# Hardware loops on VectorE, ScalarE and GpSimd, and attention probabilities staged four pairs at a time, in a decode kernel that streams a key and value cache

## The chip, the cores and the metric

One core of one Trainium2 chip runs the whole program. The metric is the device time in microseconds of one execution; where several runs are given, the median.

## The reference

Two token rows go through a gated mix of a cached attention (32 heads of 128, 4096 cached positions, batch 2) and a small feed-forward network. Cut to what matters:

```python
q = (x @ wq)                                      # [2, 32 heads, 1, 128]
scores = einsum("bhqd,bhkd->bhqk", q, k) * Dh**-0.5
p = softmax(scores)
o = einsum("bhqk,bhkd->bhqd", p, v)               # k, v: [2, 32, 4096, 128] bf16, 67 MB each
a = o.reshape(B, Sq, Hq * Dh) @ wo
b = relu(x @ w1) @ w2
return g * a + (1 - g) * b                        # g = sigmoid(sum(x * gate_w))
```

The caches are 134 MB of the 145 MB that the kernel reads; each byte is used once.

## The kernel before

One queue, issued by SyncE, loads everything in order: `wq`, `w1`, `w2`, then 32 loads of K of 2 MB (two heads of one batch row, called a pair here), 32 loads of V, and last `wo` in five pieces. K and V go through four slots:

```python
for n in range(64):
    waits = []
    if n >= NSLOT:                                   # NSLOT = 4
        prev = n - NSLOT
        waits.append(f"T_{prev}_7" if prev < 32 else f"pv_{prev - 32}")
    load(f"ld_kv_{n}", kv_sb[:, n % NSLOT, :, :], kv_in(n), waits=waits, sem=f"slot{n % NSLOT}")
```

In the K stage PE transposes each pair (64 blocks, 8 to a PSUM bank), VectorE and ScalarE evict the banks (copy them from PSUM to SBUF), and PE forms scores. In the V stage the probabilities are copied to SBUF (staged), PE multiplies them with V, and VectorE normalises. PE's two stages are already hardware loops. The other engines' instructions are written out in full:

```python
def evac(i):                                         # called for each of the 32 pairs
    p = i % PER
    for q in range(8):
        ...
        w = [f"T_{i}_{q}"] + ([f"sc_{i - NKT}"] if i >= NKT else [])
        if q in (1, 3, 5):
            P.add("act", lambda e, dst=dst, src=src: e.activation(out=dst, in_=src, func=ACT.Copy), waits=w, ...)
        else:
            P.add("dve", lambda e, dst=dst, src=src: e.tensor_copy(out=dst, in_=src), waits=w, ...)

def stage_p(i):                                      # the same, for each pair
    ...
    for hh in range(2):
        P.add("dve", lambda e, hh=hh: e.tensor_copy(out=pst[64 * hh:64 * hh + 64, p, :, hh], in_=src[:, :, 2 * hp + hh]),
              waits=[f"pt_{g}", "c_ps"] + ([f"pv_{i - PER}"] if i >= PER else []),
              signal=f"pst_{i}" if hh else None, sem=f"ps{p}")

def o_norm(i):
    ...
    P.add("dve", lambda e: e.tensor_tensor(out=oT[:, g, 2 * hp:2 * hp + 2], in0=o_col(i % PER), in1=rg[...], op=ALU.mult),
          waits=[f"pv_{i}", f"rg_{g}"], signal=f"oT_{i}", sem=f"on{i % PER}")
```

VectorE's program has 405 instructions, 107 of them waits that stand as instructions of their own; ScalarE's has 113, GpSimd's 95, PE's 1951.

Of the kernel before, what the change touches and what calls it, by code (L numbers as in the profile page):

```python
# [37 lines left out]
class _Prog:  # L38
# [7 lines left out]
    def __init__(self, nc):  # L46
        self.nc = nc
        self.streams = {e: [] for e in self.ENGINES}
        self.sems = {}
        self.marks = {}  # L50
        self.loops = []

    def sem(self, name):
        if name not in self.sems:
# [2 lines left out]

    def add(self, engine, fn, waits=(), signal=None, sem=None, inc=1):
        op = _Op(fn, waits, signal, sem or engine + "_ev", inc)
        if engine == "pe" and self.loops:  # L60
            self.loops[-1].ops.append(op)
        else:
            self.streams[engine].append(op)

    def begin_loop(self, n):
        loop = _Loop(n)
        (self.loops[-1].ops if self.loops else self.streams["pe"]).append(loop)
        self.loops.append(loop)

    def end_loop(self):  # L70
        self.loops.pop()

    def _count(self, op, name, counts):
        if name is None:
# [40 lines left out]
    def emit(self, engine, eng, items=None, iv=None, total=1):  # L115
        vals = {}
        for it in self.streams[engine] if items is None else items:
            if isinstance(it, _Loop):
                with eng.Fori(0, it.n) as k:
                    self.emit(engine, eng, it.ops, k if iv is None else iv * it.n + k, total * it.n)  # L120
                continue
            if iv is None:
                waits = list(self._needs(it.waits).items())
            else:
                waits = []
                for s, a, b in self._linear(it, total):
                    if b and (a, b) not in vals:
                        vals[(a, b)] = eng.snap(iv * b + a)
                    waits.append((s, vals[(a, b)] if b else a))
            for s, v in waits:  # L130
                eng.wait_ge(self.sem(s), v)
            ins = it.fn(eng)
            if it.signal is not None:
                ins.then_inc(self.sem(it.sem), it.inc)


def bass_gated_mix__gqa_block_cached__dense_activation_relu__decode_kernel(
# [43 lines left out]
    negM = sb("negM", [128, 2], f32)  # L181
    l4 = sb("l4", [128, 2], f32)
    lm = sb("lm", [128, 32], f32)
    rinv = sb("rinv", [128, 2, 32], f32)
    rg = sb("rg", [128, 2, 32], f32)
    oT = sb("oT", [128, 2, 32], b16)
    oA = sb("oA", [128, 2, 32, 4], b16)
    os_sb = sb("os_sb", [128, 32, 2], b16)
    f_sb = sb("f_sb", [98, 128], f32)
# [21 lines left out]
        return bank(ACC, 0, 128, 32 * c, 32 * c + 2)  # L211

    def o_col(p):
        return bank(4 + p % 2, 256 + 2 * p, 2)

    def p_place(r):

# [27 lines left out]
    for n in range(64):  # L245
        waits = []
        if n >= NSLOT:
            prev = n - NSLOT
            waits.append(f"T_{prev}_7" if prev < 32 else f"pv_{prev - 32}")
        load(f"ld_kv_{n}", kv_sb[:, n % NSLOT, :, :], kv_in(n), waits=waits, sem=f"slot{n % NSLOT}")  # L250
    WO_CUTS = (0, 16, 24, 28, 30, 32)
    for k in range(5):
# [58 lines left out]
    def T(p, qs):  # L311
        for q in qs:
            for rr in range(8):
                r = 8 * q + rr

                def waits(t, q=q):
# [4 lines left out]
                    elif p:  # L321
                        w.append(f"ev_{i - 1}_{q + 4}")
                    return w + (["qm_0", "qm_1", "f_sb"] if p == 0 and q == 0 else [])

                P.add("pe", lambda e, q=q, rr=rr, r=r: e.transpose(bank16(4 + q % 4, rr * 128, 128), kv_sb[:, p, r, :], ident16[:, :]),  # L325
                      waits=waits if rr == 0 else [],
                      signal=(lambda t, q=q: f"T_{PER * t + p}_{q}") if rr == 7 else None)

    def Sc(p):
        for c in range(8):  # L330
            for hh in range(2):
                def waits(t, c=c):
                    i = PER * t + p
                    return ([f"qst_{i}"] if c == 0 else []) + ([f"ev_{i}_{c}"] if c >= 4 else [])

                P.add("pe", lambda e, c=c, hh=hh: e.matmul(  # L336
                    S_chunk(p % 2, c), lhsT=qst[:, p, hh, :], rhs=kt_sb[:, p % NKT, 8 * c:8 * c + 8, 64 * hh:64 * hh + 64],
                    start=False, stop=True, tile_position=(0, 32 * (c % 4)), skip_group_check=True),
                    waits=waits if hh == 0 else [],
                    signal=(lambda t: f"sc_{PER * t + p}") if (c, hh) == (7, 1) else None)  # L340

    def evac(i):
        p = i % PER
        for q in range(8):
            src = bank16(4 + q % 4, 0, 1024).rearrange("p (r c) -> p r c", r=8)
            dst = kt_sb[:, p % NKT, 8 * q:8 * q + 8, :]
            w = [f"T_{i}_{q}"] + ([f"sc_{i - NKT}"] if i >= NKT else [])
            if q in (1, 3, 5):
                P.add("act", lambda e, dst=dst, src=src: e.activation(out=dst, in_=src, func=ACT.Copy), waits=w,  # L349
                      signal=f"ev_{i}_{q}", sem=f"ev{p}{q}")  # L350
            else:
                P.add("dve", lambda e, dst=dst, src=src: e.tensor_copy(out=dst, in_=src), waits=w, signal=f"ev_{i}_{q}", sem=f"ev{p}{q}")  # L352

    def stage_q(i):
        p = i % PER
        P.add("pool", lambda e: e.tensor_copy(out=qst[:, p, :, :], in_=qmask[:, 32 * (i % 2) + i // 2 * 2:32 * (i % 2) + i // 2 * 2 + 2, :]),  # L356
              waits=[f"qm_{i % 2}"] + ([f"sc_{i - PER}"] if i >= PER else []), signal=f"qst_{i}", sem=f"qs{p}")

    def scores():
        P.begin_loop(NIT)  # L360
        T(0, range(8))
        for p in range(PER):
            if p + 1 < PER:
                T(p + 1, range(2))
            Sc(p)
            if p + 1 < PER:
                T(p + 1, range(2, 8))
        P.end_loop()


    def row_max(g):
# [16 lines left out]

    def ptrans():
        for k in range(16):  # L390
            P.add("pe", lambda e, k=k: e.transpose(PSB[0:64, 128 * k:128 * k + 128], E_sb[:, 64 * k:64 * k + 64], ident16[:, :]),  # L391
                  waits=[] if k else (lambda g: [f"E_{g}"] + (["pst_15"] if g else [])),
                  signal=(lambda g: f"pt_{g}") if k == 15 else None)

    def denom_l(g):
# [1 line left out]
              waits=[f"E_{g}", "c_j4"] + (["lb_0"] if g else []), signal=f"lm_{g}", sem="lm")  # L397

    def denom_sum():
        P.add("pe", lambda e: e.matmul(bank(MISC, 0, 32), lhsT=ones[:, :], rhs=lm[:, :], start=True, stop=True),  # L400
              waits=lambda g: [f"lm_{g}", "c_one"] + (["rinv_0"] if g else []), signal=lambda g: f"lb_{g}")

    def denom(g):
        P.add("dve", lambda e: e.reciprocal(out=rinv[:, g, :], in_=bank(MISC, 0, 32)), waits=[f"lb_{g}"], signal=f"rinv_{g}")
        P.add("dve", lambda e: e.tensor_scalar(out=rg[:, g, :], in0=rinv[:, g, :], scalar1=g_sb[:, g:g + 1], scalar2=None, op0=ALU.mult),
              waits=[f"rinv_{g}", "g"], signal=f"rg_{g}")


    def stage_p(i):
        g, hp = divmod(i, 16)  # L410
        p = i % PER
        src = PSB[0:64, 0:2048].rearrange("p (k j) -> p k j", j=32)
        for hh in range(2):
            P.add("dve", lambda e, hh=hh: e.tensor_copy(out=pst[64 * hh:64 * hh + 64, p, :, hh], in_=src[:, :, 2 * hp + hh]),  # L414
                  waits=[f"pt_{g}", "c_ps"] + ([f"pv_{i - PER}"] if i >= PER else []),
                  signal=f"pst_{i}" if hh else None, sem=f"ps{p}")

    def o_norm(i):
        g, hp = divmod(i, 16)
        P.add("dve", lambda e: e.tensor_tensor(out=oT[:, g, 2 * hp:2 * hp + 2], in0=o_col(i % PER), in1=rg[:, g, 2 * hp:2 * hp + 2],  # L420
                                               op=ALU.mult),
              waits=[f"pv_{i}", f"rg_{g}"], signal=f"oT_{i}", sem=f"on{i % PER}")

    def PV(p):
        for r in range(64):

            def waits(t):
                i = PER * t + p
                return [f"ld_kv_{32 + i}", f"pst_{i}"] + ([f"oT_{i - 2}"] if i >= 2 else [])
            P.add("pe", lambda e, r=r, k=p_place(r): e.matmul(o_col(p), lhsT=kv_sb[:, p, r, :], rhs=pst[:, p, k, :],  # L430
                                                                    start=(r == 0), stop=(r == 63)),
                  waits=waits if r == 0 else [], signal=(lambda t: f"pv_{PER * t + p}") if r == 63 else None)


    def ffn_h():
# [28 lines left out]

    def o_spread():
        P.add("dve", lambda e: e.tensor_tensor(
            out=oA[:, :, :, :], in0=oT[:, :, :].unsqueeze(3).to_broadcast([128, 2, 32, 4]),
            in1=dmask[:, :].unsqueeze(1).unsqueeze(1).to_broadcast([128, 2, 32, 4]), op=ALU.mult),
            waits=[f"oT_{31 - k}" for k in range(4)] + ["c_d"], signal="oA")
        for b in range(2):  # L470
            P.add("pe", lambda e, b=b: e.matmul(bank(MISC, 32 * b, 32), lhsT=oA[:, b, :, :], rhs=jm16[:, :], start=True, stop=True),
                  waits=["oA", "c_j16"] if b == 0 else [], signal="os" if b else None)
# [13 lines left out]
    ffn_relu()  # L486
    ffn_f()
    scores()
    for i in range(32):
        stage_q(i)  # L490
    for i in range(32):
        evac(i)
    row_max(0)
    exps(0)
    denom_l(0)
    P.begin_loop(2)
    ptrans()
    denom_sum()
    P.begin_loop(4)
    for p in range(PER):  # L500
        PV(p)
    P.end_loop()
    P.end_loop()
    for g in range(2):
        for k in range(PER):
            stage_p(16 * g + k)
        denom(g)
        for i in range(16 * g, 16 * g + 16):
            o_norm(i)
            if i < 16 * g + 12:  # L510
                stage_p(i + PER)
            if i == 3:
                row_max(1)
                exps(1)
                denom_l(1)
    o_spread()
    proj()
    P.add("dve", lambda e: e.tensor_tensor(out=out_sb[:, :], in0=bank(ACC, 0, 128, 0, 98), in1=f_sb[:, :], op=ALU.add),  # L518
# [55 lines left out]
```

## Time and profile before

| | before |
|---|---|
| time, median of the first 3 runs | 350.65 us |
| span of the profiled execution | 349.2 us |
| main load queue's share of 16 DMA engines | 98.3% |
| VectorE busy | 132.8 us |

The profile of before, the page's part on DMA queues: packets, MB, and the time that their packets took as a share of the 16 engines' span.

```profile
q1 hardware_dynamic: 10488, 145.43, 98.3%
q8 instruction: 7, 0.11, 0.1%
q14 instruction: 5, 0.04, 0.0%
```

The first row is the loads. The other two, which the page calls instruction, are the engines' own programs on their way to them: q8 is PE's, q14 that of the others.

The table of windows of before: the stretch in us, its length, then busy us (and instructions) of PE, PE's weight loads, VectorE, ScalarE and GpSimd; granted clock, DMA share, GB/s.

```profile
26.00:60.00 34.00, 33.94 (x527) 29.17 (x526) 21.26 (x33) 19.42 (x20) 1.42 (x6) 1.00 1.00 425
140.00:180.00 40.00, 39.86 (x656) 32.22 (x648) 26.61 (x41) 24.32 (x25) 1.42 (x6) 1.00 1.01 429
240.00:280.00 40.00, 17.29 (x530) 16.49 (x530) 5.23 (x26) 0.00 (x0) 0.00 (x0) 0.50 1.01 429
```

The second-last number is full in K and V stage alike: the kernel is bound by its loads.

The groups of instructions of before that the change touches, and PE's products with V: busy us, mean ns of one, and the idle time before them with what ended it.

```profile
L352 DVE COPY kt_sb<-PS 128x1024 bf16<-128x1024 bf16 x160 | 105.3, 687 | 55.6 <-PE PS L325 55.6
L430 PE MATMUL PS<-pst,kv_sb 128*128 128x2 bf16 x2048 | 59.1, 165 | 87.0 <-DMA kv_sb<-in_A_v_cache_dram 84.3
L349 ACT ACTIVATE kt_sb<-PS 128x1024 bf16<-128x1024 bf16 x96 | 94.1, 1022 | 69.4 <-PE PS L325 69.4
L420 DVE TENSOR_TENSOR oT<-PS,rg 128x2 bf16<-128x2 f32 x32 | 5.1, 159 | 123.3 <-PE PS L430 123.0
L414 DVE COPY pst<-PS 64x64 bf16<-64x64 bf16 x64 | 14.4, 225 | 3.9 <-PE PS L391 2.9
```

The chain of waits of before, a stretch of the V stage: start, us, what.

```profile
239.25 17.56 DMA kv_sb<-in_A_v_cache_dram
...
258.82 18.53 DMA kv_sb<-in_A_v_cache_dram
...
279.36 17.56 DMA kv_sb<-in_A_v_cache_dram
```

A V load in this chain takes 17.56 to 17.59 us from issue to landing, with up to four loads under way (one lands every 4.89 us), from 200 us to the end of the stage, but one took 18.53.

### The profile page before, as it was taken

Reading aid. Unit: us, or ns where it says so; the run is one execution under the profiler, and the core shown is the slowest. Engines: PE = TensorE matmul, PEld = TensorE weight load, DVE = VectorE, ACT = ScalarE, POOL = GpSimd, SP = SyncE. Lnnn points to the kernel's source line nnn. Section 1 sums busy time; section 2 is a strip of 40 time slices with the busy share of each in tenths; the row PEclk is TensorE's granted clock in tenths of the full one; section 3 lists DMA queues with packets and bytes.
Section 4 is the critical chain, followed back from the end, with each engine's and each line's share of the span. In section 5 each row is a group of like instructions: output and inputs, shape, how many; then the busy total and the mean of one; then the engine's idle time right before and its main releaser. Section 6 shows DMA issues by size and latency. Waiting matters only on the chain.

```text
span 349.2 us, 10856 instructions
## 1 busy us (share of the span) xinstructions
PE 236.3 (68%) x5007; PEld 202.7 (58%) x5007; DVE 132.8 (38%) x294; ACT 99.5 (28%) x105; POOL 12.0 (3%) x52
## 2 busy tenths in 40 slices
PE   2549999999999999999995533344354433443244
PEld 0539888787888788787884532344353423443233
DVE  0104766676766676666766231110013011110010
ACT  1004656565665566555762010000000000000000
POOL 5000000000000000000000000000000000000000
PEclk9999999999999999999998555555555555555555
DMA  8999999999999999999999999999999999999993
GB/s 327 413 423 420 428 428 424 425 434 428 423 432 435 419 424 435 432 420 428 434 430 420 427 434 422 426 432 432 422 432 423 434 422 432 432 428 422 432 416 128
DMA packets 10514, 145.59 MB, mean 417 GB/s; under 512 B 1187, under 2 KB 1286, under 8 KB 1670
## 3 DMA queue, kind: packets, MB, share of 16 engines
q1 hardware_dynamic: 10488, 145.43, 98.3%
q8 instruction: 7, 0.11, 0.1%
q14 instruction: 5, 0.04, 0.0%
q10 hardware_dynamic: 14, 0.00, 0.0%
HBM read 145.43 MB, written 0.00 MB: 416 GB/s over the span
## 4 chain that ended last, share of the span: by engine, by line
PE 49%; DMA 49%; SPq 1%; issue 1%; DVE 0%
PE PS L325 35%; DMA kv_sb<-in_A_v_cache_dram 35%; PE PS L336 10%; DMA wo_sb<-in_A_wo_dram 7%; DMA kv_sb<-in_A_k_cache_dram 7%; PE PS L430 4%; SPq L237 1%; PE PS L481 0%; DVE out_sb L518 0%
## 5 line engine op out<-in xcount | busy, mean ns | idle before, releaser
L325 PEld LDWEIGHTS PS<-ident,kv_sb 128*128 128x128 bf16 x2048 | 117.4, 99 | 18.5 <-issue 14.4
L325 PE MATMUL PS<-ident,kv_sb 128*128 128x128 bf16 x2048 | 124.1, 222 | 3.7 <-DMA kv_sb<-in_A_k_cache_dram 3.3
L352 DVE COPY kt_sb<-PS 128x1024 bf16<-128x1024 bf16 x160 | 105.3, 687 | 55.6 <-PE PS L325 55.6
L430 PE MATMUL PS<-pst,kv_sb 128*128 128x2 bf16 x2048 | 59.1, 165 | 87.0 <-DMA kv_sb<-in_A_v_cache_dram 84.3
L349 ACT ACTIVATE kt_sb<-PS 128x1024 bf16<-128x1024 bf16 x96 | 94.1, 1022 | 69.4 <-PE PS L325 69.4
L430 PEld LDWEIGHTS PS<-pst,kv_sb 128*128 128x128 bf16 x2048 | 57.2, 104 | 89.1 <-issue 70.4
L420 DVE TENSOR_TENSOR oT<-PS,rg 128x2 bf16<-128x2 f32 x32 | 5.1, 159 | 123.3 <-PE PS L430 123.0
L336 PE MATMUL PS<-kt_sb,qst 128*32 128x512 bf16 x512 | 38.2, 382 | 0.0
L336 PEld LDWEIGHTS PS<-kt_sb,qst 128*32 128x32 bf16 x512 | 13.3, 95 | 12.5 <-DVE kt_sb L352 3.6
L414 DVE COPY pst<-PS 64x64 bf16<-64x64 bf16 x64 | 14.4, 225 | 3.9 <-PE PS L391 2.9
L356 POOL COPY qst<-qmask 128x64 bf16<-128x64 bf16 x32 | 7.4, 236 | 151.7 <-PE PS L336 140.8
L385 ACT ACTIVATE E_sb<-PS,negM 128x1024 bf16<-128x1024 f32 x2 | 2.2, 1113 | 17.8 <-DVE negM L380 17.8
L481 PE MATMUL PS<-wo_sb,os_sb 128*2 128x128 bf16 x128 | 4.3, 305 | 3.2 <-DMA wo_sb<-in_A_wo_dram 3.1
L301 PE MATMUL PS<-xT_sb,wq_sb 128*128 128x2 bf16 x128 | 3.6, 165 | 3.7 <-DMA wq_sb<-in_A_wq_dram 3.7
L301 PEld LDWEIGHTS PS<-xT_sb,wq_sb 128*128 128x128 bf16 x128 | 3.5, 104 | 3.8 <-DMA wq_sb<-in_A_wq_dram 3.8
L481 PEld LDWEIGHTS PS<-wo_sb,os_sb 128*2 128x2 bf16 x128 | 2.9, 112 | 4.4 <-DMA wo_sb<-in_A_wo_dram 2.2
L391 PE MATMUL PS<-ident,E_sb 128*64 128x128 bf16 x32 | 3.0, 266 | 3.5 <-ACT E_sb L385 3.3
L391 PEld LDWEIGHTS PS<-ident,E_sb 128*64 128x64 bf16 x32 | 2.6, 139 | 4.1 <-issue 4.1
L285 PE MATMUL PS<-ident,gw_sb 1*128 1x1 bf16 x4 | 0.3, 172 | 4.7 <-DMA gw_sb<-in_gate_w_dram 4.7
L306 DVE TENSOR_SCALAR qmask<-PS 128x32 bf16<-128x32 f32 x2 | 0.5, 329 | 6.9 <-PE PS L301 6.9
L518 DVE TENSOR_TENSOR out_sb<-PS,f_sb 98x128 bf16<-98x128 f32 x1 | 0.3, 291 | 7.2 <-PE PS L481 7.2
L285 PEld LDWEIGHTS PS<-ident,gw_sb 1*128 1x128 bf16 x4 | 0.2, 115 | 4.8 <-DMA gw_sb<-in_gate_w_dram 4.8
(51 smaller groups left out, 31.8 us busy)
## 6 DMA issues: line engine op xcount, KB each, us to landing
kv_sb<-in_A_k_cache_dram SPq DMA_DIRECT2D x32, 2048.0 KB, 14.4
kv_sb<-in_A_v_cache_dram SPq DMA_DIRECT2D x32, 2048.0 KB, 17.6
wq_sb<-in_A_wq_dram SPq DMA_DIRECT2D x1, 4096.0 KB, 12.2
wo_sb<-in_A_wo_dram SPq DMA_DIRECT2D x1, 2048.0 KB, 22.1
w_sb<-in_B_w_dram SPq DMA_DIRECT2D x1, 1376.0 KB, 15.1
w_sb<-in_B_w_dram SPq DMA_DIRECT2D x1, 1280.0 KB, 19.0
wo_sb<-in_A_wo_dram SPq DMA_DIRECT2D x1, 1024.0 KB, 24.1
wo_sb<-in_A_wo_dram SPq DMA_DIRECT2D x1, 512.0 KB, 24.9
```

The lines of the kernel that those rows point to most:

```text
L237: P.add(eng, lambda e: e.dma_start(dst, src), waits=waits, signal=name, sem=sem or name, inc=16)
L301: P.add("pe", lambda e, h=h, t=t: e.matmul(bank(7, 2 * h, 2), lhsT=wq_sb[:, t, h * 128:(h + 1) * 128], rhs=xT_sb[:, t, :], start=(t == 0), ...
L325: P.add("pe", lambda e, q=q, rr=rr, r=r: e.transpose(bank16(4 + q % 4, rr * 128, 128), kv_sb[:, p, r, :], ident16[:, :]), waits=waits if r ...
L336: P.add("pe", lambda e, c=c, hh=hh: e.matmul(S_chunk(p % 2, c), lhsT=qst[:, p, hh, :], rhs=kt_sb[:, p % NKT, 8 * c:8 * c + 8, 64 * hh:64 * ...
L349: P.add("act", lambda e, dst=dst, src=src: e.activation(out=dst, in_=src, func=ACT.Copy), waits=w, signal=f"ev_{i}_{q}", sem=f"ev{p}{q}")
L352: P.add("dve", lambda e, dst=dst, src=src: e.tensor_copy(out=dst, in_=src), waits=w, signal=f"ev_{i}_{q}", sem=f"ev{p}{q}")
L356: P.add("pool", lambda e: e.tensor_copy(out=qst[:, p, :, :], in_=qmask[:, 32 * (i % 2) + i // 2 * 2:32 * (i % 2) + i // 2 * 2 + 2, :]), wa ...
L391: P.add("pe", lambda e, k=k: e.transpose(PSB[0:64, 128 * k:128 * k + 128], E_sb[:, 64 * k:64 * k + 64], ident16[:, :]), waits=[] if k else ...
L414: P.add("dve", lambda e, hh=hh: e.tensor_copy(out=pst[64 * hh:64 * hh + 64, p, :, hh], in_=src[:, :, 2 * hp + hh]), waits=[f"pt_{g}", "c_p ...
L420: P.add("dve", lambda e: e.tensor_tensor(out=oT[:, g, 2 * hp:2 * hp + 2], in0=o_col(i % PER), in1=rg[:, g, 2 * hp:2 * hp + 2], op=ALU.mult ...
L430: P.add("pe", lambda e, r=r, k=p_place(r): e.matmul(o_col(p), lhsT=kv_sb[:, p, r, :], rhs=pst[:, p, k, :], start=(r == 0), stop=(r == 63)) ...
L481: P.add("pe", lambda e, r=r, c=c: e.matmul(acc(c), lhsT=os_sb[:, r, :], rhs=wo_sb[:, r, 128 * c:128 * c + 128], start=(r == 0), stop=(r == ...
```

## The change

The intent is a smaller program for the three engines: hardware loops for evictions and for the staging of queries, and in the V stage one staging copy for each head of the pairs and one normalisation for four pairs at a time, with the four results side by side in one PSUM bank. VectorE's program falls from 405 to 164 instructions, ScalarE's from 113 to 57, GpSimd's from 95 to 52; PE's stays (1948). The diff, cut to its core:

```diff
-    def evac(i):
-        p = i % PER
-        for q in range(8):
+    def evac():
+        P.begin_loop(NIT, "dve", "act")
+        for p in range(PER):
+            for q in range(8):
 ...                                     # waits and signals become functions of the loop's index
+        P.end_loop("dve", "act")
 ...
-    def stage_q(i):
+    def stage_q():
+        P.begin_loop(NIT, "pool")
 ...
     def o_col(p):
-        return bank(4 + p % 2, 256 + 2 * p, 2)
+        return bank(4, 2 * p, 2)
 ...
-    def stage_p(i):
+    def stage_p(t):
 ...
         for hh in range(2):
-            P.add("dve", lambda e, hh=hh: e.tensor_copy(out=pst[64 * hh:64 * hh + 64, p, :, hh], in_=src[:, :, 2 * hp + hh]),
-                  waits=[f"pt_{g}", "c_ps"] + ([f"pv_{i - PER}"] if i >= PER else []),
+            P.add("dve", lambda e, hh=hh: e.tensor_copy(
+                out=pst[64 * hh:64 * hh + 64, :, :, hh], in_=src.rearrange("p k (j h) -> p j k h", h=2)[:, :, :, hh]),
+                waits=[f"pt_{g}", "c_ps"] + ([f"pv_{t - 1}"] if t else []), signal=f"pst_{t}" if hh else None, sem="ps")
+
+    def o_norm(t):
+        P.add("dve", lambda e: e.tensor_tensor(out=oT[:, 8 * t:8 * t + 8], in0=bank(4, 0, 8), in1=rg[:, 8 * t:8 * t + 8], op=ALU.mult),
+              waits=[f"pv_{t}", f"rg_{t // 4}"], signal=f"oT_{t}", sem="on")
 ...
-                return [f"ld_kv_{32 + i}", f"pst_{i}"] + ([f"oT_{i - 2}"] if i >= 2 else [])
+                w = [f"ld_kv_{32 + PER * t + p}"]
+                return w if p else w + [f"pst_{t}"] + ([f"oT_{t - 1}"] if t else [])
```

More of the change, by code (lines that the diff above doesn't have):

```diff
@@ L50, in __init__ @@
         self.marks = {}
-        self.loops = []
+        self.loops = {e: [] for e in self.ENGINES}
     def sem(self, name):
@@ L59, in add, with _at, begin_loop, end_loop @@
         op = _Op(fn, waits, signal, sem or engine + "_ev", inc)
-        if engine == "pe" and self.loops:
-            self.loops[-1].ops.append(op)
-        else:
-            self.streams[engine].append(op)
-    def begin_loop(self, n):
-        loop = _Loop(n)
-        (self.loops[-1].ops if self.loops else self.streams["pe"]).append(loop)
-        self.loops.append(loop)
-    def end_loop(self):
-        self.loops.pop()
+        self._at(engine).append(op)
+    def _at(self, engine):
+        loops = self.loops[engine]
+        return loops[-1].ops if loops else self.streams[engine]
+    def begin_loop(self, n, *engines):
+        for e in engines:
+            loop = _Loop(n)
+            self._at(e).append(loop)
+            self.loops[e].append(loop)
+    def end_loop(self, *engines):
+        for e in engines:
+            self.loops[e].pop()
     def _count(self, op, name, counts):
@@ L131, in emit @@
                 eng.wait_ge(self.sem(s), v)
-            ins = it.fn(eng)
+            ins = it.fn(eng) if iv is None else it.fn(eng, iv)
             if it.signal is not None:
@@ L183, in bass_gated_mix__gqa_block_cached__dense_activation_relu__decode_kernel @@
     lm = sb("lm", [128, 32], f32)
-    rinv = sb("rinv", [128, 2, 32], f32)
-    rg = sb("rg", [128, 2, 32], f32)
-    oT = sb("oT", [128, 2, 32], b16)
+    rinv = sb("rinv", [128, 64], f32)
+    rg = sb("rg", [128, 64], f32)
+    oT = sb("oT", [128, 64], b16)
     oA = sb("oA", [128, 2, 32, 4], b16)
@@ L248, in bass_gated_mix__gqa_block_cached__dense_activation_relu__decode_kernel @@
             prev = n - NSLOT
-            waits.append(f"T_{prev}_7" if prev < 32 else f"pv_{prev - 32}")
+            waits.append(f"T_{prev}_7" if prev < 32 else f"pv_{(prev - 32) // PER}" + ("" if prev % PER == PER - 1 else f"_{prev % PER}"))
         load(f"ld_kv_{n}", kv_sb[:, n % NSLOT, :, :], kv_in(n), waits=waits, sem=f"slot{n % NSLOT}")
@@ L323, in waits @@
                     return w + (["qm_0", "qm_1", "f_sb"] if p == 0 and q == 0 else [])
-                P.add("pe", lambda e, q=q, rr=rr, r=r: e.transpose(bank16(4 + q % 4, rr * 128, 128), kv_sb[:, p, r, :], ident16[:, :]),
+                P.add("pe", lambda e, iv, q=q, rr=rr, r=r: e.transpose(bank16(4 + q % 4, rr * 128, 128), kv_sb[:, p, r, :], ident16[:, :]),
                       waits=waits if rr == 0 else [],
@@ L334, in waits @@
                     return ([f"qst_{i}"] if c == 0 else []) + ([f"ev_{i}_{c}"] if c >= 4 else [])
-                P.add("pe", lambda e, c=c, hh=hh: e.matmul(
+                P.add("pe", lambda e, iv, c=c, hh=hh: e.matmul(
                     S_chunk(p % 2, c), lhsT=qst[:, p, hh, :], rhs=kt_sb[:, p % NKT, 8 * c:8 * c + 8, 64 * hh:64 * hh + 64],
@@ L339, in Sc @@
                     waits=waits if hh == 0 else [],
-                    signal=(lambda t: f"sc_{PER * t + p}") if (c, hh) == (7, 1) else None)
-    def evac(i):
-        p = i % PER
-        for q in range(8):
-            src = bank16(4 + q % 4, 0, 1024).rearrange("p (r c) -> p r c", r=8)
-            dst = kt_sb[:, p % NKT, 8 * q:8 * q + 8, :]
-            w = [f"T_{i}_{q}"] + ([f"sc_{i - NKT}"] if i >= NKT else [])
-            if q in (1, 3, 5):
-                P.add("act", lambda e, dst=dst, src=src: e.activation(out=dst, in_=src, func=ACT.Copy), waits=w,
-                      signal=f"ev_{i}_{q}", sem=f"ev{p}{q}")
-            else:
-                P.add("dve", lambda e, dst=dst, src=src: e.tensor_copy(out=dst, in_=src), waits=w, signal=f"ev_{i}_{q}", sem=f"ev{p}{q}")
@@ L354, in stage_q, with waits, signal @@
-    def stage_q(i):
-        p = i % PER
-        P.add("pool", lambda e: e.tensor_copy(out=qst[:, p, :, :], in_=qmask[:, 32 * (i % 2) + i // 2 * 2:32 * (i % 2) + i // 2 * 2 + 2, :]),
-              waits=[f"qm_{i % 2}"] + ([f"sc_{i - PER}"] if i >= PER else []), signal=f"qst_{i}", sem=f"qs{p}")
+                    signal=(lambda t: f"sc_{PER * t + p}") if (c, hh) == (7, 1) else None, sem=f"sc{p}")
+    def evac():
+        P.begin_loop(NIT, "dve", "act")
+        for p in range(PER):
+            for q in range(8):
+                src = bank16(4 + q % 4, 0, 1024).rearrange("p (r c) -> p r c", r=8)
+                dst = kt_sb[:, p % NKT, 8 * q:8 * q + 8, :]
+                def waits(t, p=p, q=q):
+                    i = PER * t + p
+                    return [f"T_{i}_{q}"] + ([f"sc_{i - NKT}"] if i >= NKT else [])
+                def signal(t, p=p, q=q):
+                    return f"ev_{PER * t + p}_{q}"
+                if q in (1, 3, 5):
+                    P.add("act", lambda e, iv, dst=dst, src=src: e.activation(out=dst, in_=src, func=ACT.Copy), waits=waits,
+                          signal=signal, sem=f"ev{p}{q}")
+                else:
+                    P.add("dve", lambda e, iv, dst=dst, src=src: e.tensor_copy(out=dst, in_=src), waits=waits,
+                          signal=signal, sem=f"ev{p}{q}")
+        P.end_loop("dve", "act")
@@ new lines, in stage_q, with waits @@
+    def stage_q():
+        P.begin_loop(NIT, "pool")
+        for p in range(PER):
+            def waits(t, p=p):
+                i = PER * t + p
+                return [f"qm_{p % 2}"] + ([f"sc_{i - PER}"] if i >= PER else [])
+            P.add("pool", lambda e, iv, p=p: e.tensor_copy(
+                out=qst[:, p, :, :], in_=qmask[:, bass.ds(iv * 4 + (32 * (p % 2) + p // 2 * 2), 2), :]),
+                waits=waits, signal=lambda t, p=p: f"qst_{PER * t + p}", sem=f"qs{p}")
+        P.end_loop("pool")
@@ L359, in scores @@
     def scores():
-        P.begin_loop(NIT)
+        P.begin_loop(NIT, "pe")
         T(0, range(8))
@@ L367, in scores @@
                 T(p + 1, range(2, 8))
-        P.end_loop()
+        P.end_loop("pe")
     def row_max(g):
@@ L390, in ptrans @@
         for k in range(16):
-            P.add("pe", lambda e, k=k: e.transpose(PSB[0:64, 128 * k:128 * k + 128], E_sb[:, 64 * k:64 * k + 64], ident16[:, :]),
-                  waits=[] if k else (lambda g: [f"E_{g}"] + (["pst_15"] if g else [])),
+            P.add("pe", lambda e, iv, k=k: e.transpose(PSB[0:64, 128 * k:128 * k + 128], E_sb[:, 64 * k:64 * k + 64], ident16[:, :]),
+                  waits=[] if k else (lambda g: [f"E_{g}"] + (["pst_3"] if g else [])),
                   signal=(lambda g: f"pt_{g}") if k == 15 else None)
@@ L399, in denom_sum @@
     def denom_sum():
-        P.add("pe", lambda e: e.matmul(bank(MISC, 0, 32), lhsT=ones[:, :], rhs=lm[:, :], start=True, stop=True),
+        P.add("pe", lambda e, iv: e.matmul(bank(MISC, 0, 32), lhsT=ones[:, :], rhs=lm[:, :], start=True, stop=True),
               waits=lambda g: [f"lm_{g}", "c_one"] + (["rinv_0"] if g else []), signal=lambda g: f"lb_{g}")
     def denom(g):
-        P.add("dve", lambda e: e.reciprocal(out=rinv[:, g, :], in_=bank(MISC, 0, 32)), waits=[f"lb_{g}"], signal=f"rinv_{g}")
@@ L405, in denom @@
-        P.add("dve", lambda e: e.tensor_scalar(out=rg[:, g, :], in0=rinv[:, g, :], scalar1=g_sb[:, g:g + 1], scalar2=None, op0=ALU.mult),
+        P.add("dve", lambda e: e.reciprocal(out=rinv[:, 32 * g:32 * g + 32], in_=bank(MISC, 0, 32)), waits=[f"lb_{g}"], signal=f"rinv_{g}")
+        P.add("dve", lambda e: e.tensor_scalar(out=rg[:, 32 * g:32 * g + 32], in0=rinv[:, 32 * g:32 * g + 32], scalar1=g_sb[:, g:g + 1], scalar2=None, op0=ALU.mult),
               waits=[f"rinv_{g}", "g"], signal=f"rg_{g}")
-    def stage_p(i):
-        g, hp = divmod(i, 16)
-        p = i % PER
-        src = PSB[0:64, 0:2048].rearrange("p (k j) -> p k j", j=32)
+    def stage_p(t):
+        g, u = divmod(t, 4)
+        src = PSB[0:64, 0:2048].rearrange("p (k j) -> p k j", j=32)[:, :, 8 * u:8 * u + 8]
@@ L413, in stage_p @@
         for hh in range(2):
-            P.add("dve", lambda e, hh=hh: e.tensor_copy(out=pst[64 * hh:64 * hh + 64, p, :, hh], in_=src[:, :, 2 * hp + hh]),
-                  waits=[f"pt_{g}", "c_ps"] + ([f"pv_{i - PER}"] if i >= PER else []),
-                  signal=f"pst_{i}" if hh else None, sem=f"ps{p}")
-    def o_norm(i):
-        g, hp = divmod(i, 16)
-        P.add("dve", lambda e: e.tensor_tensor(out=oT[:, g, 2 * hp:2 * hp + 2], in0=o_col(i % PER), in1=rg[:, g, 2 * hp:2 * hp + 2],
-                                               op=ALU.mult),
-              waits=[f"pv_{i}", f"rg_{g}"], signal=f"oT_{i}", sem=f"on{i % PER}")
+            P.add("dve", lambda e, hh=hh: e.tensor_copy(
+                out=pst[64 * hh:64 * hh + 64, :, :, hh], in_=src.rearrange("p k (j h) -> p j k h", h=2)[:, :, :, hh]),
+                waits=[f"pt_{g}", "c_ps"] + ([f"pv_{t - 1}"] if t else []), signal=f"pst_{t}" if hh else None, sem="ps")
@@ L427, in waits @@
             def waits(t):
-                i = PER * t + p
-                return [f"ld_kv_{32 + i}", f"pst_{i}"] + ([f"oT_{i - 2}"] if i >= 2 else [])
-            P.add("pe", lambda e, r=r, k=p_place(r): e.matmul(o_col(p), lhsT=kv_sb[:, p, r, :], rhs=pst[:, p, k, :],
-                                                                    start=(r == 0), stop=(r == 63)),
-                  waits=waits if r == 0 else [], signal=(lambda t: f"pv_{PER * t + p}") if r == 63 else None)
+                w = [f"ld_kv_{32 + PER * t + p}"]
+                return w if p else w + [f"pst_{t}"] + ([f"oT_{t - 1}"] if t else [])
+            P.add("pe", lambda e, iv, r=r, k=p_place(r): e.matmul(o_col(p), lhsT=kv_sb[:, p, r, :], rhs=pst[:, p, k, :],
+                                                                  start=(r == 0), stop=(r == 63)),
+                  waits=waits if r == 0 else [],
+                  signal=(lambda t: f"pv_{t}" if p == PER - 1 else f"pv_{t}_{p}") if r == 63 else None)
     def ffn_h():
@@ L466, in o_spread @@
         P.add("dve", lambda e: e.tensor_tensor(
-            out=oA[:, :, :, :], in0=oT[:, :, :].unsqueeze(3).to_broadcast([128, 2, 32, 4]),
+            out=oA[:, :, :, :], in0=oT[:, :].rearrange("p (b h) -> p b h", b=2).unsqueeze(3).to_broadcast([128, 2, 32, 4]),
             in1=dmask[:, :].unsqueeze(1).unsqueeze(1).to_broadcast([128, 2, 32, 4]), op=ALU.mult),
-            waits=[f"oT_{31 - k}" for k in range(4)] + ["c_d"], signal="oA")
+            waits=["oT_7", "c_d"], signal="oA")
         for b in range(2):
@@ L488, in bass_gated_mix__gqa_block_cached__dense_activation_relu__decode_kernel @@
     scores()
-    for i in range(32):
-        stage_q(i)
-    for i in range(32):
-        evac(i)
+    stage_q()
+    evac()
     row_max(0)
@@ L495, in bass_gated_mix__gqa_block_cached__dense_activation_relu__decode_kernel @@
     denom_l(0)
-    P.begin_loop(2)
+    P.begin_loop(2, "pe")
     ptrans()
     denom_sum()
-    P.begin_loop(4)
+    P.begin_loop(4, "pe")
     for p in range(PER):
         PV(p)
-    P.end_loop()
-    P.end_loop()
-    for g in range(2):
-        for k in range(PER):
-            stage_p(16 * g + k)
-        denom(g)
-        for i in range(16 * g, 16 * g + 16):
-            o_norm(i)
-            if i < 16 * g + 12:
-                stage_p(i + PER)
-            if i == 3:
-                row_max(1)
-                exps(1)
-                denom_l(1)
+    P.end_loop("pe")
+    P.end_loop("pe")
+    for t in range(NIT):
+        stage_p(t)
+        if t % 4 == 0:
+            denom(t // 4)
+        if t == 0:
+            row_max(1)
+            exps(1)
+            denom_l(1)
+        o_norm(t)
     o_spread()
```

## The prediction

> **What bounds it now.** The load queue. The page gives the main DMA queue 98.3% of the 16 engines' span. In the table of windows the DMA share is 1.00 or 1.01 in every window from 10 to 340 us, at 424 to 429 GB/s. [...] No bytes are removed, so little can move unless loads are starved.
>
> The chain of waits names PE in the K stage (L325 35%), but that is order, not bound: a K load takes 14.4 us from issue to landing (DMA issues) against 4.89 us of transfer, so about three are queued.
>
> **What the change does.**
> 1. K stage: 160 VectorE evictions (687 ns) and 96 ScalarE ones (1022 ns) stay, now in hardware loops: a register add and a separate register wait each, eight back edges per engine. PE's own stream does not move. In the timeline PE takes 19.25 us for a group of four when free (4.81 a pair), against 4.89 for a load: 0.08 us of slack. The ScalarE eviction has about 0.2 us (estimated from the timeline's order) before it blocks PE, VectorE about 0.5. I expect 0 to 0.1 us a pair, at most 3 us of PE lag over the stage.
> That lag is hidden: V load 4 waits for the first PV, which ended at 191.3 us, while loads 2 and 3 were under way, the last landing at 198.1. About 6.7 us of lag is free.
> [...] VectorE's body has 62 instructions and ScalarE's 38[...]; PE's far larger K body shows only 0.06 us of issue at its back edge (chain, 48.0 us).
> 2. V stage: 64 copies of 64x64 (225 ns, 14.4 us) become 16 of 64x256, about 0.42 us each[...], 6.7 us; 32 normalisations (5.1 us) become 8, 1.3 us. VectorE falls from 132.8 to about 121 us, but it was 10 to 20% busy there. Now PE waits at each group's start for normalisation plus staging, 1.0 us after the last PV. It waits about 3.0 us for the next V load anyway (87.0 us idle before L430, 84.3 by the load). At the second batch, transposes and sums (1.6 us) plus 0.85 stay below 3.0. The first PV starts 0.4 us later, inside the 6.7.
> 3. Tail: after the last PV, projection waits for output weights from 339.3 to 341.1 us: 1.8 us free, under 0.1 added.
> 4. Instruction fetch: 12 packets in all; savings below 0.1 us.
>
> **On the critical path:** nothing, within 0.3 us.
>
> **Predicted: 350.6 us, 8 in 10 between 350.1 and 351.2.** Faster by over 2%: 0.01. Within 2%: 0.97. Slower by over 2%: 0.02.
>
> **What would show it.** Right: DMA share 1.00 in all middle windows; evictions with the same means and counts; staging x16 near 0.42 us; VectorE near 121 us; PE idle before PV still put down to V loads; the chain ending through the output weights. Wrong: DMA share below 0.98 in or just after the K stage; issue to landing of loads down to about 5 us; PE waiting on evictions at every fourth pair.
>
> **What would make it wrong.** An instruction fetch of microseconds at each back edge on VectorE or ScalarE (over 6.7 us in sum), register waits that serialise wait and eviction, or a late first eviction. A gain could only come from fewer gaps in DMA, and I see none.

225 ns of the 0.42 us was measured, the rest was my guess, and so were the 6.7 us for 16 copies and the about 121 us for VectorE that rest on it (measured: 434 ns, 6.9 and 122.9 us). The 0 to 0.1 us a pair for the loops was a guess as well. None of them enters the 350.6 us, which is about the time before (350.65) with nothing added or saved.

## The result

The changed kernel took 349.82 us (median of 6 runs, 349.43 to 349.87) against 350.63 us for the kernel before (6 runs, 350.51 to 350.77). The ratio is 0.9974, with a 95% interval of 0.9962 to 0.9987. A ratio here is the mean time of one kernel's fast runs over that of the other's of the same rounds, so not quite the ratio of the medians. The gain of 0.8 us is small but clear of noise, and the time lies below the predicted range. All outputs were correct.

The page of after, DMA queues:

```profile
q1 hardware_dynamic: 10488, 145.43, 98.6%
q8 instruction: 7, 0.11, 0.1%
q14 instruction: 2, 0.01, 0.0%
```

The table of windows of after:

```profile
26.00:60.00 34.00, 33.76 (x535) 29.00 (x536) 21.70 (x33) 19.85 (x21) 1.43 (x6) 1.00 1.01 426
140.00:180.00 40.00, 39.86 (x659) 32.35 (x656) 26.84 (x41) 24.16 (x25) 1.43 (x6) 1.00 1.01 431
240.00:280.00 40.00, 17.41 (x530) 16.46 (x530) 2.59 (x8) 0.00 (x0) 0.00 (x0) 0.50 1.01 428
```

The groups of after:

```profile
L362 DVE COPY kt_sb<-PS 128x1024 bf16<-128x1024 bf16 x160 | 105.4, 688 | 55.4 <-PE PS L328 55.4
L444 PE MATMUL PS<-pst,kv_sb 128*128 128x2 bf16 x2048 | 59.4, 165 | 84.2 <-DMA kv_sb<-in_A_v_cache_dram 81.5
L359 ACT ACTIVATE kt_sb<-PS 128x1024 bf16<-128x1024 bf16 x96 | 94.2, 1022 | 69.4 <-PE PS L328 69.4
L436 DVE TENSOR_TENSOR oT<-PS,rg 128x8 bf16<-128x8 f32 x8 | 1.3, 166 | 131.8 <-PE PS L444 131.8
L431 DVE COPY pst<-PS 64x256 bf16<-64x256 bf16 x16 | 6.9, 434 | 3.8 <-PE PS L409 3.7
```

The evictions cost what they did. Staging and normalisation fell from 19.5 to 8.2 us. PE still waits for V loads, not for VectorE. The DMA share of the windows is as full as before. So none of the computing that the change touched explains the 0.8 us. The chain of waits of after, the same stretch:

```profile
238.85 17.63 DMA kv_sb<-in_A_v_cache_dram
...
258.42 17.64 DMA kv_sb<-in_A_v_cache_dram
...
278.00 17.63 DMA kv_sb<-in_A_v_cache_dram
```

The load of 18.53 us is gone, and of the five packets of q14 two are left, and by its record one of them is of 80 bytes, at 0.1 us.

**Where the time went.** The trace keeps 16 landing times for each load, and the page counts 16 DMA engines, so I take each time for one engine's part. The parts are equal by the packet records: from 60 to 320 us the queue carried 6788 packets of 16 KB, 128 for each step of 4.89 us, or eight for each engine at 0.61 us. So one can see how far apart the engines are. The records do not name the engines, so below they are sorted, and which engine is which is judged by its rank and by how far it moves. The load of V pair 18 (load 50 in all) in the kernel before, with its neighbours, taken from these records; all in us ("step" is the time since the load before had landed):

```
load   last landing  step   how much earlier each of the 16 engines was than the slowest
 49       266.60     4.89   2.35 2.30 2.24 2.23 2.21 2.18 2.12 1.74 1.25 0.96 0.78 0.70 0.63 0.62 0.60 0.00
 50       272.45     5.85   3.31 3.25 3.20 3.19 3.17 3.13 3.07 2.69 2.21 1.93 1.75 1.66 1.59 1.58 1.56 0.00
 51       277.35     4.89   3.32 3.26 3.19 3.18 3.17 3.13 3.08 2.69 2.21 1.93 1.74 1.66 1.60 1.59 1.56 0.00
 63       336.10     4.90   3.35 3.27 3.22 3.21 3.18 3.14 3.11 2.68 2.22 1.95 1.76 1.69 1.62 1.61 1.58 0.00
```

Between loads 49 and 50 all the other engines moved away from the slowest by 0.96 us: the slowest alone lost that much. It did not get it back, with loads always queued (17.6 us from issue to landing against a step of 4.89): the gaps of load 63 are those of load 50. The DMA packets of that moment, again from the trace's records:

```
start us  end us   bytes  queue
266.728   267.340  16384  q1
267.346   267.671   8192  q14 (instructions)
267.659   268.932  16384  q1
```

Ordinary packets follow each other at 0.61 us. Behind the instruction packet of 0.33 us comes one of 1.27 us: 0.97 us are lost for 8 KB. The changed kernel has no fetch on either queue between 201 us and the last V load, which its slowest engine finished hardly later than the next ones:

```
load   last landing  step   how much earlier each of the 16 engines was than the slowest
 63       334.79     4.90   2.12 2.01 1.96 1.96 1.87 1.80 1.79 1.77 1.56 0.85 0.32 0.32 0.26 0.22 0.09 0.00
```

The last V load landed 1.31 us earlier than in the profiled run of before (336.10), and all that follows moved with it: the last piece of the output weights landed at 344.74 instead of 346.06 us. The profiled spans differ by 1.3 us, the times of the same two executions (350.95 and 349.82) by 1.1 and the medians by 0.8; what lies outside the span I did not resolve.

**Theories.** A, B and C are what the expectations below call them. A: each block of written-out code is fetched by one DMA engine, always the same one for one engine's program, in the middle of the load stream; it costs that DMA engine up to 1 us for good; and the slowest of the 16 decides the time. B: staging four pairs at a time made the V stage shorter. C: fewer fetched bytes give the load queue a little more room, as a sum over 16 engines. Also possible: loops by themselves speed up the K stage.

### The profile page after: what moved, and what is told of

The parts are those of the page before. It is cut to its first block, busy times and chain, and to the rows that moved or that the text cites. A ratio compares the mean times of both kernels' runs of the same rounds, so it can differ in the third digit from the quotient of the medians.

```text
span 347.8 us, 11294 instructions
## 1 busy us (share of the span) xinstructions
PE 237.2 (68%) x5007; PEld 202.7 (58%) x5007; DVE 122.9 (35%) x222; ACT 99.5 (29%) x105; POOL 12.1 (3%) x52
## 4 chain that ended last, share of the span: by engine, by line
PE 51%; DMA 44%; issue 1%; SPq 1%; DVE 1%; ACT 0%; DVEq 0%
PE PS L328 35%; DMA kv_sb<-in_A_v_cache_dram 30%; PE PS L339 10%; DMA wo_sb<-in_A_wo_dram 7%; DMA kv_sb<-in_A_k_cache_dram 7%; PE PS L444 5%; SPq L240 1%; PE PS L409 1%; ACT E_sb L403 0%; DVE m L390 0%; DVE kt_sb L362 0%; DVE mq L393 0%; DVE negM L398 0%; DVE pst L431 0%; PE PS L496 0%
## 5 line engine op out<-in xcount | busy, mean ns | idle before, releaser
L444 PE MATMUL PS<-pst,kv_sb 128*128 128x2 bf16 x2048 | 59.4, 165 | 84.2 <-DMA kv_sb<-in_A_v_cache_dram 81.5
L359 ACT ACTIVATE kt_sb<-PS 128x1024 bf16<-128x1024 bf16 x96 | 94.2, 1022 | 69.4 <-PE PS L328 69.4
L436 DVE TENSOR_TENSOR oT<-PS,rg 128x8 bf16<-128x8 f32 x8 | 1.3, 166 | 131.8 <-PE PS L444 131.8
L372 POOL COPY qst<-qmask 128x64 bf16 x32 | 7.5, 238 | 151.8 <-PE PS L339 140.7
L431 DVE COPY pst<-PS 64x256 bf16<-64x256 bf16 x16 | 6.9, 434 | 3.8 <-PE PS L409 3.7
L409 PE MATMUL PS<-ident,E_sb 128*64 128x128 bf16 x32 | 3.8, 314 | 3.5 <-ACT E_sb L403 3.3
L409 PEld LDWEIGHTS PS<-ident,E_sb 128*64 128x64 bf16 x32 | 3.3, 173 | 4.1 <-issue 4.1
## 6 DMA issues: line engine op xcount, KB each, us to landing
kv_sb<-in_A_v_cache_dram SPq DMA_DIRECT2D x32, 2048.0 KB, 17.6
```

The source lines that it names most:

```text
L359: P.add("act", lambda e, iv, dst=dst, src=src: e.activation(out=dst, in_=src, func=ACT.Copy), waits=waits, signal=signal, sem=f"ev{p}{q}")
L372: P.add("pool", lambda e, iv, p=p: e.tensor_copy(out=qst[:, p, :, :], in_=qmask[:, bass.ds(iv * 4 + (32 * (p % 2) + p // 2 * 2), 2), :]), ...
L409: P.add("pe", lambda e, iv, k=k: e.transpose(PSB[0:64, 128 * k:128 * k + 128], E_sb[:, 64 * k:64 * k + 64], ident16[:, :]), waits=[] if k ...
L444: P.add("pe", lambda e, iv, r=r, k=p_place(r): e.matmul(o_col(p), lhsT=kv_sb[:, p, r, :], rhs=pst[:, p, k, :], start=(r == 0), stop=(r == ...
```

## The experiments

All were timed in five rounds against the kernel before on the same chip and were correct. They ran in three sets, each on a chip of its own (thin, stage4, dve_loop and ap_loop; then pad_dve2, pad_pool4, pad_ap2 and pe_short; then pad_dve1 and pad_dve4, planned with the second set's results). The kernel before took 350.62 to 350.78 us in them, so differences of times across sets are good to about 0.2 us; the ratios are within a set. "Fetches" are the packets of q14 while loads ran, by start in us; "lag" is by how much the slowest engine's part of the last V load came after the second slowest's. Fetches and landings are from the one profiled execution, times are medians.

| kernel | VectorE instructions | fetches of q14, us | last V landing, us | lag, us | time, us | ratio to before |
|---|---|---|---|---|---|---|
| before | 405 | 63, 93, 116, 193, 267 | 336.10 | 1.58 | 350.63 | |
| after | 164 | 46 | 334.79 | 0.09 | 349.82 | 0.9974 |
| thin | 312 | 63, 93, 116, 191 | 334.79 | 0.31 | 349.94 | 0.9977 |
| stage4 | 260 | 63, 93, 116, 193 | 334.95 | 0.21 | 349.80 | 0.9971 |
| dve_loop | 289 | 93, 116, 187, 265 | 334.99 | 0.31 | 349.75 | 0.9969 |
| ap_loop | 405 | 63, 194, 267 | 335.65 | 0.99 | 350.70 | 1.0001 |
| pad_dve1 | 292 | 45, 211 | 335.08 | 0.26 | 350.12 | 0.9983 |
| pad_dve2 | 420 | 45, 211, 231 | 335.97 | 1.15 | 351.02 | 1.0006 |
| pad_dve4 | 676 | 45, 212, 230, 250, 273 | 337.79 | 3.20 | 352.83 | 1.0059 |
| pad_pool4 | 164 | 45, 171, 183, 194, 205 | 335.41 | 0.81 | 350.44 | 0.9994 |
| pad_ap2 | 164 | 45, 171, 183, 198, 208 | 334.63 | 0.05 | 349.85 | 0.9973 |
| pe_short | 164 | 82 | 367.41 | 0.42 | 382.39 | 1.0891 |

### thin: take out needless waits, nothing else

```diff
-                  waits=[f"pt_{g}", "c_ps"] + ([f"pv_{i - PER}"] if i >= PER else []),
+                  waits=[] if hh else [f"pt_{g}"] + (["c_ps"] if i == 0 else []) + ([f"pv_{i - PER}"] if i >= PER else []),
 ...
-              waits=[f"pv_{i}", f"rg_{g}"], ...
+              waits=[f"pv_{i}"] + ([f"rg_{g}"] if hp == 0 else []), ...
```

> The kernel before, with 93 VectorE wait instructions taken out of the V stage that wait for what is already met (405 VectorE instructions become 312); no loop, no staging by four, same data work. Theory A (each block of straight-line VectorE code is fetched by one DMA engine in the middle of the load stream, costs that engine about 0.97 us that it never recovers, and the slowest of the 16 engines decides the end): the fetch seen at 267 us in the trace of before, which hit the slowest engine, goes; 349.5 to 349.9 us, and the spread of the landings of the last V load falls from 3.35 to about 2.4 us. Theory B (staging four pairs at a time shortens the V stage): 350.6 us. Theory C (what counts is the sum of all fetched bytes over 16 engines): 350.5 to 350.6 us.

Measured: 349.94 us, 0.04 above theory A's range, ratio 0.9977 (0.9963 to 0.9991). The fetch near 267 us is gone. The chain of waits of thin in the V stage:

```profile
258.44 17.58 DMA kv_sb<-in_A_v_cache_dram
```

No load stands out any more, and the spread of the last V load fell from 3.35 to 2.13 us (2.4 expected). This kernel has no new loop and stages per pair; it only has 93 instructions fewer that wait for what is already met. It gives nearly the whole gain of the change. Theory B cannot explain it, and C's 0.1 us is too little.

### stage4, dve_loop, ap_loop: the parts of the change alone

`stage4` is the changed kernel with `evac` and `stage_q` of before, without loops on the three engines. `dve_loop` and `ap_loop` are the kernel before with loops on one side: `dve_loop` on VectorE's evictions alone (below), `ap_loop` on ScalarE's evictions and GpSimd's `stage_q`, with VectorE's evictions written out as before. Both also drop VectorE's wait for the scores before an eviction; ap_loop has that edit too and is no faster than before.

```diff
+    def evac_dve():
+        P.begin_loop(NIT, "dve")
+        for p in range(PER):
+            for q in (0, 2, 4, 6, 7):
+                ...
+        P.end_loop("dve")
```

> The staging and normalising by four pairs in one bank alone, without any loop on VectorE, ScalarE or GpSimd (260 VectorE instructions). Theory A: the 267 us fetch goes, one or two VectorE fetches stay, 349.5 to 349.9 us. Theory B: 349.8 us, the whole gain. Theory C: 350.5 us.

> The kernel before with a hardware loop on VectorE's evictions alone, staging per pair as before (289 VectorE instructions). Theory A: one fetch fewer on the slowest engine, 349.5 to 349.9 us. Theory B: 350.6 us, as the V stage is unchanged. Theory C: 350.5 us.

> Loops on ScalarE and GpSimd alone; VectorE keeps its 405 instructions and the staging per pair. Theory A: the fetches at 93 and 116 us go, which hit engines that were not the slowest, so the time stays at 350.5 to 350.8 us. Theory B: 350.6 us. A theory that loops by themselves speed up the K stage: about 350.2 us.

Measured: 349.80, 349.75 and 350.70 us. Either half of what was done to VectorE gives the gain by itself, and together (the changed kernel) they give no more. The loops on ScalarE and GpSimd give nothing (ratio 1.0001, 0.9987 to 1.0015), although they take away two fetches from the middle of the loads, those at 93 and 116 us, and stage4 takes away only one. The page of ap_loop and its chain of waits:

```profile
q14 instruction: 3, 0.02, 0.0%
```

```profile
238.79 17.57 DMA kv_sb<-in_A_v_cache_dram
...
258.37 18.52 DMA kv_sb<-in_A_v_cache_dram
...
278.90 17.60 DMA kv_sb<-in_A_v_cache_dram
```

The load of 18.5 us is back, with the fetch at 267 us, and the slowest engine lags by 0.99 us. So the fetches at 63, 193 and 267 us are VectorE's (dve_loop moved or removed them, thin and stage4 took the last), and they delay one and the same engine: to judge by the ranks in the landing records of before, the engine that lost about 1 us at 63 us stood 0.38 us ahead of the slowest before 193 us, then became the slowest by 0.60 us, and after 267 us by 1.56. dve_loop still has a fetch at 265 us, but there the engine was 0.68 us ahead, and so only about 0.3 of its loss of 1 us showed.

### pad_dve1, pad_dve2, pad_dve4: give VectorE idle code back

The changed kernel, with blocks of 128 idle instructions on VectorE in the V stage, where in the changed kernel it waits 18.5 to 18.6 us before the normalisation of groups 1 to 3, and 15.9 us in group 4:

```diff
+    def pad(engine, n):
+        for _ in range(n):                           # n = 256 gave 128 instructions
+            P.add(engine, lambda e: e.wait_ge(P.sem("ld_wq"), 16))
 ...
+        if 1 <= t <= K:                              # K = 1, 2, 4
+            pad("dve", 256)
         o_norm(t)
```

> The changed kernel with 128 idle instructions on VectorE in one group of the V stage: one more block. The engine that carries VectorE's fetches has 0.86 us in hand, and two more blocks cost 1.2 us. Theory A (only the slowest engine counts): 0.97 - 0.86 = 0.1 us more than the changed kernel, 349.8 to 350.1 us. A theory of a fixed price per fetch, of which two cost 1.2 us: 0.6 us more, 350.4 us.

> The changed kernel with 256 idle instructions on VectorE (waits for a semaphore that has long been reached) in two groups of the V stage, 420 VectorE instructions in all: two more fetched blocks. In the changed kernel the engine that carries VectorE's fetches landed the last V load 0.86 us before the slowest. Theory A (all of VectorE's blocks go through the same DMA engine, 0.97 us each, slowest engine decides): 2 x 0.97 - 0.86 = 1.1 us more than the changed kernel, 350.7 to 351.1 us, with the whole gain of the change lost again. Theory C (sum of all fetches over 16 engines): 0.12 us more, 349.9 us. Theory B (staging): 349.8 us, as the work is that of the changed kernel.

> The changed kernel with 512 idle instructions on VectorE, 128 in each of four groups: four more blocks. Theory A: 4 x 0.97 - 0.86 = 3.0 us more, 352.5 to 353.0 us; at 0.65 us a block, which some blocks showed with 512 instructions on GpSimd, 1.7 us more. Fixed price per fetch: 2.4 us more. Sum over 16 engines: 0.24 us more.

Measured: 350.12, 351.02 and 352.83 us, that is 0.3, 1.2 and 3.0 us above the changed kernel. There is one fetch of 8 KB for each 128 instructions added (PE's packets on q8 were of 16 KB; why they differ the runs do not tell). Two blocks take the whole gain away. The first costs less than the later ones, as its engine has something in hand (0.3 us is hardly clear of the scatter between sets, and 350.12 lies 0.02 above theory A's range, but in the trace the engine went from 0.72 us ahead to 0.3 behind); after that each block costs 0.9 us ((352.83 - 350.12) / 3). That all of them land on the same engine is seen at the last V load of pad_dve4, where one engine stands 3.20 us behind the second slowest, and the others are where they were:

```
load   last landing  step   how much earlier each of the 16 engines was than the slowest
 63       337.79     4.89   5.10 5.06 4.99 4.99 4.96 4.95 4.73 4.70 4.58 3.50 3.42 3.34 3.25 3.24 3.20 0.00
```

The pads do no work, and VectorE has time for them: this is the price of fetching alone. The page of pad_dve4 has as many packets of q14 as that of before, yet is 2.2 us slower (352.83 against the 350.62 of its own rounds), because all four late ones hit one engine:

```profile
q1 hardware_dynamic: 10488, 145.43, 97.8%
q14 instruction: 5, 0.04, 0.0%
```

### pad_pool4 and pad_ap2: the same bytes on one engine or on two

```diff
     stage_q()
+    pad("pool", 1024)        # pad_pool4: 512 instructions
+    pad("pool", 512)         # pad_ap2: 256 instructions here,
 ...
+            pad("act", 512)  #          and 256 on ScalarE after its last exponentials
```

> The changed kernel with 512 idle instructions on GpSimd after its loop: four more blocks. Theory A: GpSimd's fetches share one DMA engine, one that is about 1.8 to 2.1 us ahead of the slowest, so 4 x 0.97 - 1.95 = 1.9 us more, 351.4 to 352.0 us. Theory C: 0.24 us more, 350.05 us. If fetches were spread over different engines: 349.8 us.

> The changed kernel with 256 idle instructions on GpSimd and 256 on ScalarE: four more blocks, as many bytes as in the run with 512 on GpSimd. Theory A (each instruction stream has a DMA engine of its own): 2 x 0.97 us on each of two engines that are about 1.95 us ahead of the slowest, so 0.0 to 0.2 us more, 349.7 to 350.1 us. If both streams shared an engine: 351.4 to 352.0 us. Theory C: 350.05 us.

Measured: 350.44 us (350.35 to 350.84) and 349.85 us (349.64 to 349.95). Both fetch four more blocks than the changed kernel. Spread over two programs they cost nothing; on one program they cost 0.6 us. That decides for the slowest engine and against the sum. The size for pad_pool4 was missed: I expected 1.9 us. The records say why: each of GpSimd's four blocks cost its DMA engine 0.65 us and not 0.97 (a fetch of 0.31 us, and behind it a packet of 0.96 us instead of 0.61), 2.6 us in all instead of 3.9, and to judge by the ranks the engine was about 1.8 us ahead when it began. After three blocks it had become the slowest by 0.16 us, and after the fourth by about 0.8.

So the price of an 8 KB block is not one constant, but the packet records of all runs show that, while the load queue is full, it goes with the program: 0.97 to 0.99 us for every block of VectorE, 0.65 to 0.66 for GpSimd's six in pad_pool4 and pad_ap2, 0.68 to 0.69 for ScalarE's two in pad_ap2. What makes the programs differ is open.

### pe_short: fewer of PE's own blocks

PE's fetches, 7 packets of 16 KB on q8, are the rest of the story: in the changed kernel several engines share the last place (six within 0.32 us at the last V load), and to judge by the ranks most of them carried one such block each, at about 1.55 us by the packet records. I tried to leave some out by looping over the query projection and a feed-forward product with addresses from registers:

```diff
-    for h in range(HQ):
-        for t in range(4):
-            P.add("pe", lambda e, h=h, t=t: e.matmul(bank(7, 2 * h, 2), lhsT=wq_sb[:, t, h * 128:(h + 1) * 128], ...
+    P.begin_loop(HQ, "pe")
+    for t in range(4):
+        P.add("pe", lambda e, iv, t=t: e.matmul(PSF[:, bass.ds(iv * 2 + 3584, 2)], lhsT=wq_sb[:, t, bass.ds(iv * 128, 128)], ...
+    P.end_loop("pe")
```

> The changed kernel with hardware loops on PE for the query projection and the first feed-forward product (1948 PE instructions become 1647, about 1.2 blocks of 16 KB). In the changed kernel the slowest engines all carry one PE block each, at 1.4 to 1.6 us. Theory A: one or two of the seven PE blocks go, but the slowest engine is one of those that stay, so 349.5 to 349.9 us, within 0.3 us of the changed kernel. Theory C: 0.1 to 0.2 us less. If PE's blocks were what bounds in sum: 1.5 us less.

Measured: 382.39 us, 32.6 us more than the changed kernel, a plain failure. The page of pe_short, the group of the projection, and its table of windows:

```profile
L304 PE MATMUL PS<-xT_sb,wq_sb 128*128 128x2 bf16 x128 | 18.2, 178 | 20.9 <-issue 16.9
```

```profile
10.00:40.00 30.00, 13.64 (x96) 9.98 (x96) 0.00 (x0) 0.00 (x0) 0.00 (x0) 1.00 0.95 400
40.00:60.00 20.00, 10.91 (x76) 8.85 (x76) 0.43 (x2) 0.00 (x0) 0.85 (x4) 1.00 0.00 0
```

Each pass over four products with register addresses takes about 1.12 us in the timeline; written out, all 128 products took 3.57 us, 0.11 us for four. How much of it is the addresses and how much the loop itself was not tested. PE began the first transposes at 62.8 us instead of 26.3, all four slots were full, and from 40 to 60 us the DMA engines moved nothing. So here PE's lag of 36.5 us was too much for the four slots: the loads stopped. One of PE's seven packets did go (q8 shows 6), but the run does not tell whether fewer PE blocks would help, as the loads stopped in between; that stays open.

## Why the prediction was wrong

The prediction said 350.6 us, in a range of 350.1 to 351.2. The change gave 349.82.

- *"What bounds it now: the load queue."* Right, but too coarse. It is the slowest of the queue's 16 engines. The DMA share of 1.00 to 1.01 that I relied on is their mean; it is the same in a kernel whose slowest engine lags by 1.58 us and in one where it lags by 0.09.
- *"Instruction fetch: 12 packets in all; savings below 0.1 us."* This is the step that failed. I counted bytes against the bandwidth of all 16 engines. The fetch at 267 us occupied one engine for 0.33 us, delayed it by 0.97 us, and that was not made up in the 69 us of full queue up to the last V load. VectorE's three blocks fell on one engine; losing one of them, alone, was worth 0.7 us (thin), and the prediction allowed nothing for it.
- *"On the critical path: nothing, within 0.3 us"*, and *"a gain could only come from fewer gaps in DMA, and I see none."* Wrong in consequence. The gap was there to be seen: one V load of 18.53 us among loads of 17.56 in the chain.
- *K stage:* right. Evictions took 688 and 1022 ns (687 and 1022 before). DMA stayed full, and ap_loop and dve_loop show no cost of the loops' register waits and back edges (ratios to before 1.0001 and 0.9969). The fetch at each back edge that the prediction named as a risk did not come: after 45.8 us, no queue of instruction packets shows a fetch before 194.5 us in after.
- *V stage:* right. Staging took 434 ns (0.42 us predicted), VectorE 122.9 us in all (121 predicted), and PE's wait before V products is still the load's, 81.5 of 84.2 us. The first product started at 190.89 us instead of 189.43, 1.5 us later and not 0.4 (in part because the 16 probability transposes took 1.9 us, not 1.1); it was hidden in the loads under way, as argued.
- *Tail:* right. Projection waited from 337.9 to 339.8 us for output weights.

## What to carry to other kernels

When a kernel is bound by loads that are split evenly over all DMA engines, look at the landing times of the single engines and not at the mean share: in these runs, what delayed the slowest engine once delayed the end (pad_dve4: 3.20 us of lag, 3.0 us more time). Straight-line code on a side engine was such a delay: each 128 instructions more, even waits that were long met, cost an 8 KB fetch that took 0.65 to 0.99 us from one engine, and all fetches of VectorE hit the same one, and all of GpSimd's in pad_pool4. Shortening code paid only for the program whose engine was the slowest (thin 0.7 us, ap_loop nothing), and only down to the next slowest (both halves of what was done to VectorE together gave 0.8 us, no more than stage4 or dve_loop alone).

No version beat the changed kernel clearly: thin, stage4 and dve_loop tie with it. To judge by the ranks, VectorE's engine is still the slowest in these three, but only by 0.2 to 0.3 us; in the changed kernel it is 0.85 us ahead, and an engine that carries a block of PE's is the slowest.
